# A decode-step kernel on one core: the last row of w2 brought in for 80 of its 128 partitions by two transfers of 40

## The chip, the cores and the metric

The kernel runs on one core of one Trainium2 chip. The metric is the device time of one execution in microseconds (us). The kernel before the change takes 133.50 us, the median of three runs (133.49, 133.50 and 133.52). Smaller is better.

## What is computed

Two branches read the same layer-normalized vector and are added to the input. Branch A is attention for one new token per batch row (B = 2) over the last 2048 positions of a cache; branch B is a dense layer with a squared ReLU. Cut to what matters:

```python
xn = _layernorm(x)                       # x: (2, 1, 576)
# A: 32 query heads, 16 kv heads, head size 128, window W = 2048
q = xn @ wq                              # wq: 576 x 4096
p = softmax(q . k[Sk-W:] * Dh**-0.5)
A = (p . v[Sk-W:]) @ wo                  # wo: 4096 x 576
# B: F = 4608
r = relu(xn @ w1 + b1)                   # w1: 576 x 4608
Bo = (r * r) @ w2 + b2                   # w2: 4608 x 576
return x + A + Bo
```

All inputs are bf16. The k and v windows and the four weight matrices make 53.6 MB, which have to be read from memory once.

## The kernel before

**The work and its stages.** The 2 x 16 cached heads are worked off as eight units (`NU`) of four kv heads each; unit u takes head group `u // 2` of batch row `u % 2`. A unit needs one k tile and one v tile, each 128 partitions by 8192 elements (2 MB). They sit in a pool of six buffers (`kvpool`, tag `kv`), so that a load waits until PE has finished with an older tile. `step(u)` (line 388) transposes k on PE in eight groups of four matmuls (`transposes`, line 261; ACT and DVE take turns copying the result to SBUF, lines 273 and 275), forms the scores, takes the softmax, and in between multiplies the probabilities of unit u - 2 with v (`pv`, line 315). Before the steps the kernel normalizes x, loads wq and forms q (`q_rows`, `q_place`). After step 6 `mlp_h` (line 357) forms h from w1, squares its ReLU, and transposes it: 18 small PE transposes into `hp`, and eight copies of 32 partitions, shared by DVE and ACT, into `hT_sb` (lines 379 to 386). Then come the last step (unit 7), the last two `pv`, and the output products.

**The output products.** `wo` and `w2` are laid over the 128 partitions so that each partition holds whole rows. For w2, line 208 gives half x, partition p and row r: `w2_rows[x, p, r]` is row x*2304 + 18*p + r of w2, 576 numbers. A product for one r is therefore a pair of PE matmuls (`out_acc`, line 216, one for each half of the 576 columns) with the 128 x 2 activations `hT_sb[:, x, r, :]` as weights and the 128 x 288 pieces of w2 as data, summed in PSUM (`out_ps`). The first half of w2 is `w2a` (18 rows). The second half is `w2b` (rows 0 to 8, in a buffer of the kv pool) and `w2c` (rows 9 to 17), which line 76 cuts into three transfers: rows 9 to 14 (864 KB), rows 15 and 16 (288 KB) and row 17 (144 KB). The final loop (line 468) takes the 18 pairs in order; after row 8 it has three matmuls on `spin_ps` whose result is used by nobody.

**What sets the order.** All big loads are issued by SP, in the order of the program text, and every transfer of 128 partitions lies on all 16 DMA engines, 8 partitions on each. `keep_in_program_order` (lines 93 and 96) holds PE to the order of the text, so a PE instruction that waits holds up all that come behind it. DVE, ACT and POOL are ordered by the tile scheduler. Each DMA counts on one of eight semaphores in turn, and its issue waits for the transfer that used the semaphore before. ACT issues the small loads: x (line 126), b1 in two transfers of four rows (line 420) and b2 (line 421). At the end ACT copies the sum out of PSUM (line 478), and ACT and SP each write half of the result (lines 479 and 480). Ahead of that, line 477 lets ACT write two rows of w2b into the output, which the real write overwrites later.

Of the kernel before, what the change touches and what calls it, by code (L numbers as in the profile page):

```python
# [8 lines left out]
F32 = mybir.dt.float32  # L9
BF16 = mybir.dt.bfloat16  # L10
# [6 lines left out]
def kernel(  # L17
# [14 lines left out]
    nc = tc.nc  # L32
    P = 128
    B, Sq, D = A_x.shape
# [39 lines left out]
    FR = L1 // P  # L74
    assert HW == 32 * FR and QH * 2 == NC and NC * WC == 32
    W2P = [(9, 15), (15, 17), (17, 18)]
    R9 = 9
    HD = D // 2
    RO = 32 + B
    RP = 96 + B  # L80
# [3 lines left out]
    kvpool = ctx.enter_context(tc.tile_pool(name="kvpool", bufs=6))  # L84
# [3 lines left out]
    work = ctx.enter_context(tc.tile_pool(name="work", bufs=2))  # L88
    keep = ctx.enter_context(tc.tile_pool(name="keep", bufs=2))
    psum = ctx.enter_context(tc.tile_pool(name="psum", bufs=1, space=bass.MemoryType.PSUM))  # L90

    def matmul(*a, **k):
        tc.keep_in_program_order(nc.tensor.matmul(*a, **k))  # L93
# [5 lines left out]
    out2d = out.rearrange("b s d -> (b s) d")  # L99
# [50 lines left out]
    ident = const.tile([P, P], BF16, name="ident")  # L150
# [29 lines left out]
    for t0, half, k0, n, pc in ((0, 0, 0, NK, 0), (0, 1, 0, NK, 1), (1, 0, 1, NK - 1, 1), (1, 1, 0, NK - 1, 0)):  # L180
# [11 lines left out]
                          in_=own[:].unsqueeze(2).to_broadcast([P, NC, WC]))  # L192
    in_s = const.tile([P, NS], F32, name="in_s")
    nc.vector.tensor_reduce(out=in_s[:], in_=ident[:].rearrange("p (g s c) -> p s g c", s=NS, c=NC), axis=AX.XY,
                            op=ALU.add)
# [8 lines left out]
                          in_=ident[0:2 * NG4, 0:2 * NG4].rearrange("p (x g) -> p x g", g=NG4).unsqueeze(3)  # L204
                          .to_broadcast([2 * NG4, 2, NG4, B]))

    b1_sb = const.tile([2 * NG4, HW], BF16, name="b1_sb")
    w2_rows = B_w2.rearrange("(x p r) n -> x p (r n)", x=2, r=FR)


    w2c_sb = w2pool.tile([P, (FR - R9) * D], BF16, name="w2c")

    out_ps = psum.tile([RO, HD], F32, tag="out", name="out_ps")
    nc.vector.memset(out_ps[:], 0.0)

    def out_acc(lhsT, rhs, o, start=False, stop=False, acc=out_ps, base=0):
        for i in range(2):
            p = base + 32 * i
            matmul(acc[p:p + B, :], lhsT=lhsT, rhs=rhs[:, o * D + i * HD:o * D + (i + 1) * HD], start=start,
                   stop=stop, skip_group_check=True, tile_position=(0, p))  # L220
# [40 lines left out]
    def transposes(u, g):  # L261
        k_f = k_tiles[u][:].bitcast(F32)
        kT_ps = psum.tile([P, JG * P], BF16, tag="kT", bufs=3, name=f"kT_ps_{u}_{g}")
        kT_f = kT_ps[:].bitcast(F32)
        for i in range(JG // 2):
            j = g * JG // 2 + i
            transpose(out=kT_f[:, i * P:(i + 1) * P], in_=k_f[:, j * P:(j + 1) * P], identity=ident_f[:])
        t, o = divmod(g, TG)
        if o == 0:
            kT_tiles[(u, t)] = ktpool.tile([P, TG * JG * P], BF16, tag="kT_sb", name=f"kT_{u}_{t}")  # L270
        kT = kT_tiles[(u, t)][:, o * JG * P:(o + 1) * JG * P]
        if g % 2 == 0:
            nc.scalar.copy(out=kT, in_=kT_ps[:])  # L273
        else:
            nc.vector.tensor_copy(out=kT, in_=kT_ps[:])  # L275
# [35 lines left out]

    ws = const.tile([P, WR, B], BF16, name="ws")
    hT_sb = const.tile([P, 2, FR, B], BF16, name="hT_sb")

    def pv(u, part, parts):
        n = NJJ // parts
        if part == 0:
            o_tiles[u] = psum.tile([P, NS * Dh], F32, tag="o", name=f"o_ps_{u}")
        v = v_tiles[u][:].rearrange("p (t j s d) -> p j t s d", t=NT, s=2, d=Dh)
        for j in range(part * n, (part + 1) * n):  # L320
            g = j % 4
            matmul(o_tiles[u][32 * g:32 * (g + 1), :], lhsT=pT_tiles[u][:, j, :], rhs=v[:, j], start=(j < 4),
                   stop=(j >= NJJ - 4), skip_group_check=True, tile_position=(0, 32 * g))
        if part == parts - 1:
            pT_tiles.pop(u)

    def pv_end(u):
        tq, b = divmod(u, B)
        o_ps = o_tiles.pop(u)
        o1 = o1_tiles.pop(u)  # L330
        for k in range(NS):
            kw = dict(out=o1[:, 0:Dh], in0=o_ps[:, k * Dh:(k + 1) * Dh])
            if k == 0:
                nc.vector.tensor_scalar(scalar1=in_s[:, 0:1], scalar2=None, op0=ALU.mult, **kw)  # L334
            else:
                nc.vector.scalar_tensor_tensor(scalar=in_s[:, k:k + 1], in1=o1[:, 0:Dh], op0=ALU.mult, op1=ALU.add,  # L336
                                               **kw)

        def fin():
            op = psum.tile([P, Dh + 1], F32, tag="op", name=f"op_ps_{u}")  # L340
            pp = slice(32 * tq, 32 * (tq + 1))
            matmul(op[pp, :], lhsT=of_h[:], rhs=o1[:], start=True, stop=True, skip_group_check=True,
                   tile_position=(0, 32 * tq))
            linv = work.tile([P, 1], F32, tag="linv", name=f"linv_{u}")
            nc.vector.reciprocal(out=linv[pp, :], in_=op[pp, Dh:Dh + 1])
            om_t = work.tile([P, Dh], F32, tag="om", name=f"om_{u}")
            om = om_t[pp, :].rearrange("p (q r) -> p q r", r=WR)
            nc.vector.scalar_tensor_tensor(out=om, in0=op[pp, 0:Dh].rearrange("p (q r) -> p q r", r=WR),
                                           scalar=linv[pp, 0:1], op0=ALU.mult, op1=ALU.mult,
                                           in1=own_c[pp, :].unsqueeze(2).to_broadcast([32, WC, WR]))  # L350
            with nc.allow_low_precision(reason="sums of one term and zeros"):
                nc.vector.tensor_reduce(out=ws[pp, :, b], in_=om.rearrange("p q r -> p r q"), axis=AX.X,  # L352
                                        op=ALU.add)

        return fin

    def mlp_h(w1_sb):
# [20 lines left out]
        for a in range(2):  # L378
# [3 lines left out]
            for g in range(NG4):  # L382
# [2 lines left out]
                cp(out=hT_sb[pp, :, a * nr:(a + 1) * nr, :].rearrange("p x r b -> p r x b"),  # L385
                   in_=hp[pp, :, 32 * g:32 * g + 2 * B].rearrange("p r (x b) -> p r x b", b=B))

    def step(u):
        fin = None
        w = u - 2  # L390
        with_pv = w >= 0
        for g in range(NG):
            transposes(u, g)
            if with_pv and g == 1:
                pv(w, 0, 2)
            if with_pv and g == 2:
                pv(w, 1, 2)
                fin = pv_end(w)
            if g == TG + 1:
                scores(u, 0)  # L400
            if g == TG + 2 and fin:
                fin()
        scores(u, 1)
        softmax(u)

    def pv_all(u):
        pv(u, 0, 1)
        pv_end(u)()
# [7 lines left out]
    softmax(0)  # L416
    load_v(2)
    b1_rows = B_b1.rearrange("(x n) -> x n", n=HW)
    for i0, i1 in ((0, 4), (4, 8)):
        nc.scalar.dma_start(out=b1_sb[i0:i1, :], in_=b1_rows[i0:i1, :])  # L420
    nc.scalar.dma_start(out=xb_sb[B:B + 1, :], in_=B_b2.rearrange("(o n) -> o n", o=1))
    step(1)
    load_k(4)
    out_acc(sel_b[:], xb_sb, 0, start=True)
    for u in range(2, NU - 1):
        step(u)
        if u + 1 < NU - 2:
            load_v(u + 1)
        if u == 4:
            w1_sb = issue_flat(B_w1, "w1")  # L430
        if u + 3 < NU:
            load_k(u + 3)
        if u == 5:
            for v in (NU - 2, NU - 1):
                load_v(v)
    mlp_h(w1_sb)
    wo_sb = issue_flat(A_wo, "wo")
    w2a_sb = w2pool.tile([P, FR * D], BF16, name="w2a")
    w2b_sb = kvpool.tile([P, R9 * D], BF16, tag="kv", name="w2b")
    nc.sync.dma_start(out=w2a_sb[:], in_=w2_rows[0])  # L440
    nc.sync.dma_start(out=w2b_sb[:], in_=w2_rows[1, :, 0:R9 * D])
    for r0, r1 in W2P:
        nc.sync.dma_start(out=w2c_sb[:, (r0 - R9) * D:(r1 - R9) * D], in_=w2_rows[1, :, r0 * D:r1 * D])
    step(NU - 1)
    pv_all(NU - 2)
    pv_all(NU - 1)
    pre_ps = psum.tile([RP, HD], F32, tag="sc", bufs=2, name="pre_ps")
    nc.vector.memset(pre_ps[:], 0.0)
    pre_sb = work.tile([P, HD], F32, tag="t1", name="pre_sb")
    nc.gpsimd.memset(pre_sb[:], 0.0)  # L450
# [13 lines left out]
    for i in range(2):  # L464
        p = 64 + 32 * i
        matmul(out_ps[32 * i:32 * i + B, :], lhsT=ident_f[:, p:p + B], rhs=pre_sb[:], start=False, stop=False,
               skip_group_check=True, tile_position=(0, 32 * i))
    for r in range(FR):
        w, o = (w2b_sb, r) if r < R9 else (w2c_sb, r - R9)
        out_acc(hT_sb[:, 1, r, :], w, o, stop=(r == FR - 1))  # L470
        if r == R9 - 1:
            for _ in range(3):
                matmul(spin_ps[0:B, :], lhsT=ws[:, 0, :], rhs=wo_sb[:, 0:512], start=True, stop=True,
                       skip_group_check=True)

    fin_sb = work.tile([RO, HD], BF16, tag="fin", name="fin_sb")
    nc.scalar.dma_start(out=out2d[:, 0:HD], in_=w2b_sb[0:B, 0:HD])
    nc.scalar.copy(out=fin_sb[:], in_=out_ps[:])
    nc.scalar.dma_start(out=out2d[:, 0:HD], in_=fin_sb[0:B, :])
    nc.sync.dma_start(out=out2d[:, HD:D], in_=fin_sb[32:RO, :])  # L480
# [30 lines left out]
```

## Time and profile before

| | us |
|---|---|
| median of three runs | 133.50 |
| the profiled execution, its time | 133.6 |
| its span, first to last instruction | 131.7 |
| PE busy (matmuls) | 84.6 |
| DVE busy | 63.1 |
| ACT busy | 46.6 |
| mean granted clock of TensorE | 0.883 |
| DMA, MB and mean rate over the span | 53.74 MB, 408 GB/s |

The profile is of one execution. Busy times are shares of the span; matmuls are pipelined, so that their busy time overlaps. "PEld" is the load of weights into TensorE. In the chain of waits each piece is what the next one waited for; a DMA piece in it runs from the issue to the landing, so it holds the time in the queue behind earlier transfers too. The windows view gives for a stretch of time the busy time of an engine, the granted clock (1.00 is full speed) and the mean busy share of the 16 DMA engines. The trace also keeps the start, length and size of every DMA packet, and the moment at which each engine's part of a transfer was counted on its semaphore.

### The profile page before, as it was taken

What the parts mean: (1) busy time and instruction counts of PE and PEld (TensorE: products, weight loads), DVE (VectorE), ACT (ScalarE), POOL (GpSimd) and SP (SyncE); (2) the same over time, 40 slices, a digit from 0 to 9 for tenths busy, and PEclk for the clock granted to TensorE, in tenths of its full rate; (3) what the DMA queues carried; (4) which work ended last, traced back from release to release, by engine and by line L of the source; (5) the groups of instructions that cost most, each with busy time, mean ns of one, the idle gap of its engine ahead of it and who ended that gap; (6) DMA issues with size and microseconds to landing.
All of it is one profiled execution on the core that took longest, in us unless ns stands there. A gap on an engine that the chain in (4) does not pass through costs nothing.

```text
span 131.7 us, 2025 instructions
## 1 busy us (share of the span) xinstructions
PE 84.6 (64%) x818; PEld 46.3 (35%) x818; DVE 63.1 (48%) x176; ACT 46.6 (35%) x68; POOL 4.2 (3%) x14
## 2 busy tenths in 40 slices
PE   0040767985599687699687797003919974629782
PEld 0010236553346353345353353002507631205341
DVE  6760034555447677457677496400073487560000
ACT  6700019497255185265085283200015452000101
POOL 2000000010100100100100100100010001000000
PEclk9999999999779999859999999955586899655799
DMA  4999999999999999999999999999999989899970
GB/s 118 480 419 420 418 443 418 448 418 423 445 413 438 423 443 428 413 458 413 443 423 411 458 490 403 408 431 428 413 443 418 504 381 504 382 416 403 400 286 1
DMA packets 3643, 53.74 MB, mean 408 GB/s; under 512 B 418, under 2 KB 563, under 8 KB 819
## 3 DMA queue, kind: packets, MB, share of 16 engines
q1 hardware_dynamic: 3604, 53.61, 95.6%
q8 instruction: 6, 0.10, 0.3%
q10 hardware_dynamic: 30, 0.02, 0.0%
q14 instruction: 3, 0.02, 0.0%
HBM read 53.62 MB, written 0.00 MB: 407 GB/s over the span
## 4 chain that ended last, share of the span: by engine, by line
DMA 74%; PE 15%; ACT 5%; issue 1%; SPq 1%; DVE 1%; ACTq 0%; DVEq 0%
DMA w<-in_B_w_dram 24%; DMA w2c<-in_B_w_dram 23%; DMA k<-in_A_k_cache_dram 17%; DMA wq<-in_A_wq_dram 10%; PE kT_ps L96 5%; PE h_ps L93 3%; ACT kT L273 3%; PE q_ps L93 2%; PE sc_ps L93 2%; PE o_ps L93 1%; PE out_ps L93 1%; ACT L305 1%; SPq L120 1%; DVE qrow L241 1%; ACT qrow L241 0%
## 5 line engine op out<-in xcount | busy, mean ns | idle before, releaser
L96 PE MATMUL kT_ps<-ident_f,k 128*128 128x128 f32 x256 | 39.0, 295 | 6.7 <-DMA k<-in_A_k_cache_dram 4.2
L273 ACT COPY kT<-kT_ps 128x1024 bf16<-128x1024 bf16 x32 | 31.8, 1012 | 15.3 <-PE kT_ps L96 15.3
L96 PEld LDWEIGHTS kT_ps<-ident_f,k 128*128 128x128 f32 x256 | 29.3, 149 | 21.8 <-issue 7.4
L275 DVE COPY kT<-kT_ps 128x1024 bf16<-128x1024 bf16 x32 | 21.8, 682 | 6.4 <-PE kT_ps L96 5.9
L93 PE MATMUL sc_ps<-kT,qz 128*32 128x512 bf16 x128 | 9.8, 384 | 6.1 <-DVE kT L275 5.5
L305 ACT ACTIVATE p<-sc_ps,bias 128x512 bf16<-128x512 f32 x8 | 5.5, 687 | 21.5 <-DVE gown L301 21.4
L93 PE MATMUL o_ps<-v,pT 128*32 128x512 bf16 x128 | 12.2, 466 | 0.0
L93 PE MATMUL h_ps<-w,xnT 128*4 128x288 bf16 x72 | 4.5, 442 | 8.8 <-DMA w<-in_B_w_dram 8.8
L93 PEld LDWEIGHTS <-xnT 128*4 128x4 bf16 x108 | 3.5, 117 | 18.3 <-issue 15.3
L336 DVE SCALAR_TENSOR_TENSOR o<-o_ps,in_s,o 128x128 f32<-128x128 f32 x24 | 8.2, 344 | 0.4
L308 DVE STREAM_TRANSPOSE pT<-p 128x512 bf16<-128x512 bf16 x8 | 5.7, 709 | 5.6 <-ACT p L305 5.6
L376 DVE TENSOR_TENSOR hrow<-t 100x1152 bf16<-100x1152 f32 x2 | 2.6, 1354 | 10.5 <-ACT t L374 10.5
L93 PE MATMUL q_ps<-wq,xnT 128*4 128x512 bf16 x36 | 4.2, 622 | 5.4 <-DMA wq<-in_A_wq_dram 4.0
L294 DVE TENSOR_REDUCE m<-sc_ps 128x1 f32<-128x512 f32 x8 | 5.5, 691 | 3.4 <-PE sc_ps L93 3.4
L93 PE MATMUL op_ps<-o,of_h 128*32 128x129 f32 x16 | 3.4, 299 | 4.6 <-DVE o L336 4.6
L298 POOL PARTITION_ALL_REDUCE gmax<-m x8 | 2.9, 365 | 92.2 <-DVE m L296 92.2
L93 PEld LDWEIGHTS <-qz 128*32 128x32 bf16 x128 | 2.0, 94 | 9.9 <-DVE kT L275 7.6
L334 DVE TENSOR_SCALAR o<-o_ps,in_s 128x128 f32<-128x128 f32 x8 | 2.7, 343 | 5.3 <-PE o_ps L93 5.3
L96 PE MATMUL pro_ps<-ident,xn_sb 2*128 2x2 bf16 x5 | 0.9, 181 | 6.8 <-DVE xn_sb L171 6.5
L241 ACT CAST qrow<-q_ps 100x512 bf16<-100x512 f32 x1 | 0.6, 585 | 12.1 <-DVE qrow L241 12.1
L463 ACT COPY pre_sb<-pre_ps 34x288 f32<-34x288 f32 x1 | 0.4, 393 | 12.6 <-PE pre_ps L93 12.6
L93 PE MATMUL out_ps<-wo,ws 128*2 128x288 bf16 x32 | 4.0, 441 | 1.1 <-DVE ws L352 1.1
(76 smaller groups left out, 61.4 us busy)
## 6 DMA issues: line engine op xcount, KB each, us to landing
k<-in_A_k_cache_dram SPq DMA_DIRECT2D x8, 2048.0 KB, 25.6
v<-in_A_v_cache_dram SPq DMA_DIRECT2D x8, 2048.0 KB, 22.8
w<-in_B_w_dram SPq DMA_DIRECT2D x1, 5184.0 KB
wo<-in_A_wo_dram SPq DMA_DIRECT2D x1, 4608.0 KB
wq<-in_A_wq_dram SPq DMA_DIRECT2D x1, 3584.0 KB, 12.9
w2a<-in_B_w_dram SPq DMA_DIRECT2D x1, 2592.0 KB
w2b<-in_B_w_dram SPq DMA_DIRECT2D x1, 1296.0 KB, 29.2
wq<-in_A_wq_dram SPq DMA_DIRECT2D x1, 1024.0 KB, 4.8
```

The lines of the kernel that those rows point to most:

```text
L93: tc.keep_in_program_order(nc.tensor.matmul(*a, **k))
L96: tc.keep_in_program_order(nc.tensor.transpose(*a, **k))
L241: cp(out=qrow[:, k * QW:(k + 1) * QW].rearrange("p (i a d) -> p i a d", a=2, d=Dh), in_=q_ps[0:RB, k * QW // 2:(k + 1) * QW // 2].rearrang ...
L273: nc.scalar.copy(out=kT, in_=kT_ps[:])
L275: nc.vector.tensor_copy(out=kT, in_=kT_ps[:])
L294: nc.vector.tensor_reduce(out=m1[:], in_=sc_ps[:], axis=AX.X, op=ALU.max)
L298: nc.gpsimd.partition_all_reduce(gmax[:], m2[:], channels=P, reduce_op=ReduceOp.max)
L305: nc.scalar.activation(out=p_sb[:], in_=sc_ps[:], func=ACT.Exp, bias=bias[:, 0:1], scale=scale, accum_out=o1[:, Dh:Dh + 1])
L308: nc.vector.transpose(out=pT[:].rearrange("p j r -> p (j r)"), in_=p_sb[:])
L334: nc.vector.tensor_scalar(scalar1=in_s[:, 0:1], scalar2=None, op0=ALU.mult, **kw)
L336: nc.vector.scalar_tensor_tensor(scalar=in_s[:, k:k + 1], in1=o1[:, 0:Dh], op0=ALU.mult, op1=ALU.add, **kw)
L376: nc.vector.tensor_tensor(out=h4[:, :, k * HB:(k + 1) * HB], in0=t4, in1=t4, op=ALU.mult)
```

## The change

Row 17 of the second half of w2 no longer arrives in one transfer of 128 partitions. Partitions 80 to 127 (48 of them) are still loaded into `w2c`; the other 80 rows are brought by two transfers of 40 into partitions 0 to 39 of a spare place at the end of `w2b` (`w2s_sb`). Their source is walked as 5 groups of 8 partitions that lie 16 apart. Both are issued ahead of the transfer of rows 15 and 16. The activations have to follow: two 0/1 matrices (`pick`, cut from the identity) move the 80 activations of row 17 to partitions 0 to 39 (`hs_ps`, two PE products at the end of `mlp_h`, then a DVE copy to `hs_sb`). The final loop gets two more pairs of matmuls ahead of row 15, for `hs_sb`; the pair of row 17 remains with all 128 partitions, and its 80 unloaded ones are set to zero by POOL at the start. b1 is loaded by one transfer of 8 rows in place of two of 4, and the early write of line 477 is gone.

```diff
+    GS = 5
+    PS = 8 * GS
+    nc.gpsimd.memset(w2c_sb[0:2 * PS, (FR - R9 - 1) * D:], 0.0)
...
+    hs_sb = work.tile([PS, 2, B], BF16, tag="hs", bufs=1, name="hs_sb")
+    pick = work.tile([P, 2, PS], BF16, tag="pick", bufs=1, name="pick")
+    nc.vector.tensor_copy(out=pick[:].rearrange("p s (g i) -> p s g i", g=GS),
+                          in_=ident[:, 0:2 * PS].rearrange("p (g s i) -> p s g i", g=GS, s=2))
...
+        hs_ps = psum.tile([PS, 2, B], F32, tag="op", name="hs_ps")
+        for i in range(2):
+            matmul(hs_ps[:, i, :], lhsT=pick[:, i, :], rhs=hT_sb[:, 1, FR - 1, :], start=True, stop=True, skip_group_check=True)
+        nc.vector.tensor_copy(out=hs_sb[:], in_=hs_ps[:])
...
-    for i0, i1 in ((0, 4), (4, 8)):
-        nc.scalar.dma_start(out=b1_sb[i0:i1, :], in_=b1_rows[i0:i1, :])
+    nc.scalar.dma_start(out=b1_sb[:], in_=b1_rows[:, :])
...
-    w2b_sb = kvpool.tile([P, R9 * D], BF16, tag="kv", name="w2b")
+    w2b_sb = kvpool.tile([P, (R9 + 2) * D], BF16, tag="kv", name="w2b")
+    w2s_sb = w2b_sb[0:PS, R9 * D:]
...
     for r0, r1 in W2P:
-        nc.sync.dma_start(out=w2c_sb[:, (r0 - R9) * D:(r1 - R9) * D], in_=w2_rows[1, :, r0 * D:r1 * D])
+        p0 = 2 * PS if r1 == FR else 0
+        if r1 == FR - 1:
+            src = w2_rows[1, 0:2 * PS, r1 * D:].rearrange("(g s i) n -> s g i n", g=GS, s=2)
+            for i in range(2):
+                nc.sync.dma_start(out=w2s_sb[:, i * D:(i + 1) * D], in_=src[i])
+        nc.sync.dma_start(out=w2c_sb[p0:, (r0 - R9) * D:(r1 - R9) * D], in_=w2_rows[1, p0:, r0 * D:r1 * D])
...
         w, o = (w2b_sb, r) if r < R9 else (w2c_sb, r - R9)
+        if r == W2P[1][0]:
+            for i in range(2):
+                out_acc(hs_sb[:, i, :], w2s_sb, i)
         out_acc(hT_sb[:, 1, r, :], w, o, stop=(r == FR - 1))
...
-    nc.scalar.dma_start(out=out2d[:, 0:HD], in_=w2b_sb[0:B, 0:HD])
```

More of the change, by code (lines that the diff above doesn't have):

```diff
@@ L438 @@
     w2a_sb = w2pool.tile([P, FR * D], BF16, name="w2a")
-    w2b_sb = kvpool.tile([P, R9 * D], BF16, tag="kv", name="w2b")
+    w2b_sb = kvpool.tile([P, (R9 + 2) * D], BF16, tag="kv", name="w2b")
+    w2s_sb = w2b_sb[0:PS, R9 * D:]
     nc.sync.dma_start(out=w2a_sb[:], in_=w2_rows[0])
-    nc.sync.dma_start(out=w2b_sb[:], in_=w2_rows[1, :, 0:R9 * D])
+    nc.sync.dma_start(out=w2b_sb[:, 0:R9 * D], in_=w2_rows[1, :, 0:R9 * D])
     for r0, r1 in W2P:
-        nc.sync.dma_start(out=w2c_sb[:, (r0 - R9) * D:(r1 - R9) * D], in_=w2_rows[1, :, r0 * D:r1 * D])
+        p0 = 2 * PS if r1 == FR else 0
[4 more added lines that the diff above has]
+        nc.sync.dma_start(out=w2c_sb[p0:, (r0 - R9) * D:(r1 - R9) * D], in_=w2_rows[1, p0:, r0 * D:r1 * D])
     step(NU - 1)
```

## The prediction, on record before the changed kernel ran

> **What bounds the kernel now.** I read the page first, then the chain of waits, then the windows of the last microseconds. The page has the DMA engines full from start to end, and the chain that ended last is mostly DMA:
>
> ```profile
> DMA  4999999999999999999999999999999989899970
> ...
> q8 instruction: 6, 0.10, 0.3%
> q10 hardware_dynamic: 30, 0.02, 0.0%
> ...
> DMA 74%; PE 15%; ACT 5%; issue 1%; SPq 1%; DVE 1%; ACTq 0%; DVEq 0%
> ```
>
> So nothing on PE, ACT or DVE counts before the last bytes of w2 arrive, unless it makes PE late for them. The end of the chain of waits:
>
> ```profile
> 96.95 30.81 DMA w2c<-in_B_w_dram
> 127.75 0.04 issue
> 127.80 1.36 PE out_ps L93 x18
> 129.16 0.02 issue
> 129.18 0.39 ACT fin_sb L478
> ```
>
> The landing that the end hangs on is that of the **first** piece of w2c (rows 9 to 14), at 127.75; from there PE runs its nine pairs (x18) nearly without a break. Timelines cut to one engine show how nearly (a group is listed whole, or from the window's first instruction on):
>
> ```profile
> 125.73 1.27 PE L93 MATMUL out_ps<-w2b,hT_sb 128*2 128x288 bf16 x18 [0.21 <-DMA w2b<-in_B_w_dram]
> 126.83 0.81 PE L93 MATMUL spin_ps<-wo,ws 128*2 128x512 bf16 x3
> 127.80 0.29 PE L93 MATMUL out_ps<-w2c,hT_sb 128*2 128x288 bf16 x2 [0.15 <-DMA w2c<-in_B_w_dram]
> 128.85 0.29 PE L93 MATMUL out_ps<-w2c,hT_sb 128*2 128x288 bf16 x2
> ```
>
> Nine pairs on w2b, all landed, take 1.27 with 0.283 for the last pair alone: (1.27 - 0.283) / 8 = 0.123 from pair to pair. At that pace the pair of row 17, eight after row 9, would start at 127.80 + 0.98 = 128.78. It started at 128.85. **The wait for the transfer that the change cuts up is worth 0.07 to 0.08 us**, no more. Its landing count in the trace is complete at 128.81.
>
> Why does it land that late? The windows view (us, PE busy, granted clock, DMA share, GB/s):
>
> ```profile
> 126.40:126.80 0.40, 0.40 (x10) 1.00 0.99 379
> 126.80:127.20 0.40, 0.40 (x6) 1.00 0.53 210
> 127.20:127.60 0.40, 0.40 (x3) 1.00 0.48 180
> 127.60:128.00 0.40, 0.24 (x5) 1.00 0.38 147
> 128.00:128.40 0.40, 0.40 (x10) 1.00 0.29 104
> 128.40:128.80 0.40, 0.40 (x10) 1.00 0.01 3
> ```
>
> The 16 engines don't end together: 0.53 is some eight engines, 0.29 some five. Following the packets (each starts where the last one of its engine ends) gives the ends of row 17: eight engines at 126.66 to 127.05, two at 127.54 and 127.59, six at 128.09, 128.24, 128.31, 128.43, 128.44 and 128.49. The late ones are those that also carried instruction fetches: the six 16 KB packets of q8 (started at 28.9, 48.6, 68.2, 83.0, 105.0, 123.3) hit six different engines and put each some 1.5 behind; two 8 KB packets of q14 put two others 0.75 behind.
>
> **The change, part by part.** *DMA.* A packet of one 1152-byte row starts 0.047 after the one before. Late engines not used by the 40-row transfers carry 3 rows of row 17 in place of 8: 5 x 0.047 = 0.235 less, so 128.49 becomes 128.25 and the landing 128.81 becomes 128.58. An engine that takes 8 rows of each 40-row transfer carries 16 + 3 in place of 8, and two more count packets: 11 x 0.047 + 0.012 = 0.53 more. How many engines these transfers use, no row shows. The nearest: a transfer of 128 rows ends with 16 count packets, one for each engine used, and ACT's transfers of 1, 2 and 4 rows (q10) with 1, 2 and 4; so the ends are one engine (80 x 0.047 = 3.8 us on it) and sixteen (nothing won, nothing lost). I take five engines with 8 rows each, as the source is walked as five groups of eight, the way four rows went to four engines; the four that the b1 transfers used ended at 126.77, 126.83, 127.54 and 127.59, so plus 0.53 they end by 128.12, still inside the others. [...]
>
> *PE's tail.* Two more pairs ahead of row 15: 2 x 0.123 = 0.245. Row 9 starts at 127.80 as before, since nothing ahead of the first w2c piece is changed; its six pairs end their starts as before, the two new ones follow, rows 15 and 16, and row 17 starts at 127.80 + 10 x 0.123 = 129.03, with its landing (128.58) long past. Before it was 128.85: **+0.17**. That the new pairs have 40 partitions instead of 128 I count as nothing, since PE streams 288 columns either way. They wait for the two small transfers, which follow the first w2c piece: on an engine that ended it at 126.49 their 16 rows end by 127.3, plus 0.35 from packet to count 127.6; cover 0.9 before 128.53.
>
> *PE at the end of `mlp_h`.* The two small products wait for all eight copies into hT_sb, and unit 7's transposes stand behind them. Before, those began at 99.69, while the copies ran until 100.56 (DVE) and one ACT copy came at 101.90, behind a kT copy; in the new order ACT has it ahead, so at about 100.6. With two products of 0.1 to 0.2 the transposes start near 101.0: 1.3 late. At that point the clock is half; from 103.01 it was full, so work pushed past it takes half as long, and 0.65 remains. Again from 118.4 to 123.5 (half clock, wo products): 0.65 shrinks to about 0.3. PE's waits further on are 0.25 (w2a), 0.21 (w2b) and 0.15 (w2c): cost 0. Without that cover up to 1.3.
>
> *The rest.* pick: about 0.2 (DVE copies and compares of that width take 0.16 to 0.29) in DVE's 0.68 idle ahead of rstd: 0. The POOL memset, between 0.34 (pre_sb) and 0.74 (qz), pushes the qz memset to about 2.0; qz is first written by DVE at 19.2: 0. hs_sb's copy, 0.18 like hT_sb's, ahead of a kT copy for which DVE waited 1.1: 0. SP issues two more transfers (0.43 each) and by the turn of semaphores the last one waits for a later v tile; all that is 15 us and more before their bytes are due: 0. b1 in one transfer: ACT issues one less, first use at 91: 0, and at most 0.06 on an engine. The dropped write: ACT stood idle from there to 129.18: 0; if it had warmed the path, the last ACT issue (0.25) might take SP's 0.32, and SP's half lands last anyway.
>
> **Sum.** Profiled execution 133.6 = span 131.7 + 1.9 around it; +0.17 gives 133.77. The median is 0.1 below the profiled execution, so 133.50 + 0.17 = 133.67, **133.7**. What a measurement of this kernel can tell from no change is about 0.2%, 0.27 us: I forecast a small loss inside that.
>
> **Rivals.**
> 1. *The late transfer was the bound after all: faster.* For: q1 alone fills 95.6% of the 16 engines over the span (page, part 3). Against: the wait before row 17 is 0.08, and the landing at 127.75, with eight pairs behind it, is untouched. With the new pairs hidden the most is -0.08, 133.4; for -0.27 the first w2c piece too would have to land 0.4 earlier, on all six late engines (they ended it at 126.99 to 127.38). 0.08.
> 2. *The fifth engine is a late one: slower.* By the count above four engines are known and none is of the six late; of the other twelve, half are. Then its row 17 ends 0.53 later, 128.6 to 129.0, counts 0.35 later, and PE starts 0.04 after: 129.0 to 129.4 against 128.85, so +0.17 to +0.56, mostly +0.5: 134.0. It decides as soon as that engine ends row 17 after 128.6. If the fetches go round the engines in turn, the fifth is less likely hit than a coin toss: 0.25.
> 3. *The small transfers hinder other engines.* They write partitions 0 to 39, which in the large transfers belong to several engines. If two engines that write neighbouring partitions share a way in, each of up to 8 packets steals 0.047 from a late engine still on the first w2c piece: +0.38 on 127.75, with the 0.17 133.5 + 0.55 = 134.05. Nothing in the trace shows such sharing. [...] 0.10.
> 4. *PE comes late* from the stall in `mlp_h`. If the clock stays half from 103.0 to 106.4 (it rose after windows with PE busy 2.81 of 3.41 and more, not after 2.30; here about 2.5), 1.3 stays, and with the waits above 0.1 to 0.3 may reach the end: 133.9. 0.07.
>
> **Numbers.** Forecast 0.50, rivals 0.08, 0.25, 0.10, 0.07. The range leaves out half of rival 1 and the upper ends of 2 and 3: 133.45 to 134.1. Faster by over 0.2%: 0.08. Within: 0.50 and the lowest part of rival 2, 0.52. Slower: 0.40.
>
> **What would show it.** Right: the last windows empty earlier, no wait before row 17, 22 matmuls from 127.8 at 0.123 a pair, the cast 0.17 later. The stall: unit 7's transposes from 101.0, wo products from 118.4 to 119.5, w2b still begun on its landing. Rival 2: a wait before row 15 or 17; rival 3: the first w2c piece landing after 127.9. Wrong altogether: that first landing moving by more than 0.1 either way.

## The result: 134.44 us, 0.7% slower, and the profile after

The changed kernel takes 134.44 us (median of six runs, 134.17 to 134.80) against 133.50: ratio 1.0072, interval 1.0055 to 1.0088. The forecast was 133.7, with a range up to 134.1. The profiled execution took 134.39, its span is 132.4. Each trace below is of one execution, and the six runs lie 0.6 apart, so a tenth read from a single trace is no more than that trace's.

The end of the chain of waits (start, length, what), which before was one DMA piece and PE's last pairs, now lies on PE throughout:

```profile
125.38 0.40 ACT pre_sb L480
125.78 0.04 issue
125.83 1.76 PE out_ps L95 x22
127.58 0.64 PE spin_ps L95 x3
128.22 1.55 PE out_ps L95 x22
129.78 0.02 issue
129.80 0.39 ACT fin_sb L497
```

ACT's cast starts at 129.80, 0.62 later than before. PE's timeline of the same stretch:

```profile
126.31 1.27 PE L95 MATMUL out_ps<-w2b,hT_sb 128*2 128x288 bf16 x18
127.41 0.81 PE L95 MATMUL spin_ps<-wo,ws 128*2 128x512 bf16 x3
128.02 0.94 PE L95 MATMUL out_ps<-w2c,hT_sb 128*2 128x288 bf16 x12
128.89 0.41 PE L95 MATMUL out_ps<-w2b,hs_sb 40*2 40x288 bf16 x4
129.23 0.53 PE L95 MATMUL out_ps<-w2c,hT_sb 128*2 128x288 bf16 x6
```

No line has an idle time behind it: PE never waits here. It comes to w2b at 126.31, 0.62 after that landed (125.69 in the trace); before, it waited for it and began at 125.73. And the landing of the first w2c piece, counted complete at 127.75 before, is now at 127.98. PE gets there at the same moment, so two separate delays meet in one start, 128.02 instead of 127.80. From there the pairs run with two breaks: the six pairs of rows 9 to 14 would give way after 0.74, at 128.76, but the pairs with 40 partitions start at 128.89, and row 15 at 129.23 and not at 129.14. (Of the first break's 0.13, 0.04 belongs to the last spin: the second matmul of row 9's pair begins only at 128.06. In the kernels below, where PE waits for the landing, this break is 0.09 to 0.10.) Row 17 no longer waits.

The same windows as before (us, PE busy, granted clock, DMA share, GB/s):

```profile
126.40:126.80 0.40, 0.40 (x10) 1.00 0.85 277
126.80:127.20 0.40, 0.40 (x12) 1.00 0.57 199
127.20:127.60 0.40, 0.40 (x9) 1.00 0.68 231
127.60:128.00 0.40, 0.40 (x3) 1.00 0.50 196
128.00:128.40 0.40, 0.40 (x9) 1.00 0.22 75
128.40:128.80 0.40, 0.40 (x10) 1.00 0.00 0
```

The last window is empty, as forecast. But from 127.2 to 127.6 the engines are more busy than before (0.68 against 0.48) and move fewer bytes for it: 231/0.68 = 340 GB/s at full share, before 180/0.48 = 375. Some packets take longer, which the packet records show one by one (below).

**The account of the profiled executions**, 134.39 - 133.6 = 0.79: start of the first w2c pair +0.22; two more pairs +0.245; the two breaks +0.22; the wait before row 17 -0.08; that is 0.61, and the cast is 0.62 later. The time from the last landing to the end of the span is 0.90 instead of 0.83, and what lies outside the span 1.99 instead of 1.89. The profiled execution of before is 0.10 above its median, that of after 0.05 below, which makes the rest of the 0.94.

### The profile page after: what moved, and what is told of

Read it like the earlier page. It is cut to its first block, busy times and chain, and to the rows that moved or that the text cites. A ratio compares the mean times of both kernels' runs of the same rounds, so it can differ in the third digit from the quotient of the medians.

```text
span 132.4 us, 2039 instructions
## 1 busy us (share of the span) xinstructions
PE 84.4 (64%) x824; PEld 48.2 (36%) x824; DVE 63.4 (48%) x178; ACT 46.7 (35%) x68; POOL 4.7 (4%) x15
## 4 chain that ended last, share of the span: by engine, by line
DMA 51%; PE 31%; DVE 8%; ACT 5%; issue 2%; POOLq 0%; SPq 0%; ACTq 0%
DMA w<-in_B_w_dram 25%; DMA k<-in_A_k_cache_dram 17%; PE kT_ps L98 10%; DMA wq<-in_A_wq_dram 10%; PE out_ps L95 6%; PE h_ps L95 3%; PE sc_ps L95 3%; PE q_ps L95 2%; PE o_ps L95 2%; ACT kT L276 2%; DVE hrow L383 2%; DVE o L343 2%; PE hp L98 1%; ACT L308 1%; PE op_ps L95 1%
## 5 line engine op out<-in xcount | busy, mean ns | idle before, releaser
L98 PE MATMUL kT_ps<-ident_f,k 128*128 128x128 f32 x256 | 39.8, 301 | 7.4 <-DMA k<-in_A_k_cache_dram 6.2
L98 PEld LDWEIGHTS kT_ps<-ident_f,k 128*128 128x128 f32 x256 | 30.5, 152 | 21.7 <-issue 12.6
L95 PE MATMUL o_ps<-v,pT 128*32 128x512 bf16 x128 | 11.0, 430 | 0.0
L244 DVE CAST qrow<-q_ps 100x512 bf16<-100x512 f32 x1 | 0.7, 690 | 8.2 <-PE q_ps L95 8.2
```

What stands on the lines that cost most here:

```text
L98: tc.keep_in_program_order(nc.tensor.transpose(*a, **k))
L244: cp(out=qrow[:, k * QW:(k + 1) * QW].rearrange("p (i a d) -> p i a d", a=2, d=Dh), in_=q_ps[0:RB, k * QW // 2:(k + 1) * QW // 2].rearrang ...
```

## The experiments

Theory after reading the profile: three causes. The small transfers hinder the late engines, those that are still on the first w2c piece when the others are done (rival 3 of the prediction); PE is late from `mlp_h` (rival 4), beside the first and hidden behind it; and the tail costs 0.36 in place of 0.17, because of the switch to 40 partitions and back. The rival theories: the tail alone, or the two small edits (b1, the early write). Results in one table; each ratio is to runs of the kernel before on the same chip. "Pair" is the start of the first pair on w2c, "end" the time from the last landing to the end of the span, both of the profiled execution. The profiled execution of before is 0.1 above its usual median. The runs of before beside the a kernels have a median of 133.67, those beside the others 133.48 to 133.53; the times expected below were worked out from 133.5.

| kernel | ratio, interval | first w2c landing | pair | cast | end |
|---|---|---|---|---|---|
| before | 1 | 127.75 | 127.80 | 129.18 | 0.83 |
| after | 1.0072, 1.0055 to 1.0088 | 127.98 | 128.02 | 129.80 | 0.90 |
| a1_stall | 1.0029, 1.0018 to 1.0040 | 127.68 | PE late | 129.81 | 0.82 |
| a2_dma | 1.0038, 1.0026 to 1.0051 | 128.36 | 128.40 | 129.71 | 0.90 |
| a3_pairs | 1.0098, 1.0083 to 1.0114 | 128.63 | 128.68 | 130.41 | 0.83 |
| a4_late | 1.0070, 1.0058 to 1.0083 | 128.25 | 128.29 | 130.03 | 0.89 |
| b1_misc | 1.0016, 1.0007 to 1.0025 | 127.60 | 127.64 | 129.04 | 0.96 |
| f1_nowrite | 1.0009, 1.0000 to 1.0017 | 127.63 | 127.67 | 129.07 | 0.89 |
| c1_ownpart | 1.0018, 1.0008 to 1.0027 | 128.02 | 128.06 | 129.40 | 0.93 |
| c3_pairs40 | 1.0032, 1.0019 to 1.0045 | 127.71 | 127.75 | 129.49 | 0.83 |
| c4_pairs128 | 1.0018, 1.0009 to 1.0027 | 127.64 | 127.68 | 129.24 | 0.83 |
| d1_both | 1.0057, 1.0044 to 1.0069 | 127.85 | 127.89 | 129.63 | 0.93 |
| d2_ownonly | 1.0096, 1.0081 to 1.0112 | 127.90 | 127.94 | 129.68 | 0.94 |
| e1_best | 1.0045, 1.0033 to 1.0058 | other pieces | | 129.05 | 1.09 |
| e3_three | 1.0024, 1.0014 to 1.0035 | other pieces | | 129.11 | 0.89 |
| g1_code | 1.0008, 0.9999 to 1.0017 | 127.74 | 127.78 | 129.18 | 0.83 |

### One part at a time

**a1_stall**: before, with `pick`, `hs_ps` and `hs_sb` as in the change, their result used by nobody.

```diff
...
+        hs_ps = psum.tile([PS, 2, B], F32, tag="op", name="hs_ps")
+        for i in range(2):
+            matmul(hs_ps[:, i, :], lhsT=pick[:, i, :], rhs=hT_sb[:, 1, FR - 1, :], start=True, stop=True, skip_group_check=True)
+        nc.vector.tensor_copy(out=hs_sb[:], in_=hs_ps[:])
```

> The kernel before, with the 0/1 matrices, the two small products at the end of mlp_h and their DVE copy added; nothing uses their result, transfers and output products are those of before. If PE's path is the cause (theory 1: the wait for all eight copies holds up the transposes of unit 7, and PE comes late to the first w2c piece), the transposes start at about 101.2 instead of 99.7, PE begins the w2c pairs 0.1 to 0.4 after their landing at 127.75, and the time is 133.6 to 133.9. If the small transfers on the DMA engines are the cause (theory 2), 133.5.

+0.36 (134.03 against 133.67). The transposes of unit 7 start at 101.02. PE's lines at the end:

```profile
126.27 0.65 PE L95 MATMUL out_ps<-pre_sb,ident_f 128*2 128x288 f32 x4 [0.56 <-ACT pre_sb L474]
126.75 1.27 PE L95 MATMUL out_ps<-w2b,hT_sb 128*2 128x288 bf16 x18
```

w2b had landed at 125.63, and before its pairs began at 125.73: PE is 1.0 late here, more than expected, and the spins and the wait for w2c cover only a part. The stall alone outlasts all the cover that the prediction counted on.

**a2_dma**: the change without the pick, the products and the two pairs; what remains are the transfers, b1 and the early write.

```diff
...
-        if r == W2P[1][0]:
-            for i in range(2):
-                out_acc(hs_sb[:, i, :], w2s_sb, i)
```

> The changed kernel without the 0/1 matrices, the products and the two extra pairs: the transfers, the zeroed rows, b1 and the dropped write stay, so the 80 rows of w2 are loaded but left out of the sum. Theory 1: PE arrives as before and the wait before row 17 is gone, 133.4 to 133.5. Theory 2: the first w2c piece lands at about 127.98 instead of 127.75 with packets stretched around 126.5 to 127.5, row 17 starts at 128.03 + 0.98 = 129.0, and the time is 133.65 to 133.75.

+0.49 (134.16), and a landing later than the 127.98 expected: PE is on time and waits 0.62 for the first piece, which lands at 128.36:

```profile
126.96 0.81 PE L95 MATMUL spin_ps<-wo,ws 128*2 128x512 bf16 x3
128.40 1.27 PE L95 MATMUL out_ps<-w2c,hT_sb 128*2 128x288 bf16 x18 [0.62 <-DMA w2c<-in_B_w_dram]
```

So here transfers that are queued behind the first piece delay it: it lands at 128.36, 127.75 in before. What the packet records show of it comes in the next part.

**a3_pairs**: before, with two more pairs of 40 partitions on zeros ahead of row 15, and the small `hs_sb` among the constants.

```diff
+    hs_sb = const.tile([PS, 2, B], BF16, name="hs_sb")
+    nc.gpsimd.memset(hs_sb[:], 0.0)
...
+        if r == W2P[1][0]:
+            for i in range(2):
+                out_acc(hs_sb[:, i, :], w2b_sb[0:PS, :], i)
```

> The kernel before with two extra pairs of 40 partitions ahead of row 15 (zero activations, first rows of w2b as data), all else as before. By the pace of 0.123 alone: +0.245 less the wait of 0.08, so +0.17, 133.67. With the two breaks seen at the switch between 128 and 40 partitions (0.13 and 0.09): +0.39, 133.9. Theory 2: 133.5.

134.94, far too much. Not the pairs: w1 already lands at 91.55 (before 91.04). The added constant moved every large tile by 32 bytes (w2c, for one, from address 168960 to 168992), and from 20 us on the 16 KB packets take 614 ns at the median instead of 611, some 621. It was redone as c3_pairs40.

**c3_pairs40, c4_pairs128**: the same with `hs_sb` in the work pool, which moves no large tile; once 40 partitions, once 128.

```diff
-    hs_sb = const.tile([PS, 2, B], BF16, name="hs_sb")
+    hs_sb = work.tile([PS, 2, B], BF16, tag="hs", bufs=1, name="hs_sb")
```

and for c4_pairs128 also

```diff
-    hs_sb = work.tile([PS, 2, B], BF16, tag="hs", bufs=1, name="hs_sb")
+    hs_sb = work.tile([P, 2, B], BF16, tag="hs", bufs=1, name="hs_sb")
...
-                out_acc(hs_sb[:, i, :], w2b_sb[0:PS, :], i)
+                out_acc(hs_sb[:, i, :], w2b_sb[:], i)
```

> The kernel before with two more pairs of matmuls ahead of row 15, on 40 partitions, with activations of zero and w2b as data (as a3_pairs, but the small activation tile is in the work pool and not among the constants, where it moved the places of the large tiles and every 16 KB packet took 614 ns in place of 611). Theory (switching the weights from 128 to 40 partitions and back costs PE about 0.2, the pairs 0.245, the wait for row 17 gives 0.07 back): the last matmul 0.36 to 0.39 later from the first w2c pair than before, 133.9 to 134.0; DMA as before. If the switch were free: +0.17, 133.75.

> As c3_pairs40, with the two added pairs on all 128 partitions. Theory (the switch is what breaks the pace): 22 matmuls at 0.123 us a pair without a break, +0.17, 133.75; 0.15 to 0.22 less than c3_pairs40. If the breaks belong to the change of the data tile and not to the number of partitions, it takes the same as c3_pairs40.

+0.44 and +0.20. PE's last lines, c3_pairs40 first:

```profile
127.75 0.90 PE L95 MATMUL out_ps<-w2c,hT_sb 128*2 128x288 bf16 x12 [0.15 <-DMA w2c<-in_B_w_dram]
128.58 0.41 PE L95 MATMUL out_ps<-w2b,hs_sb 40*2 40x288 bf16 x4
128.92 0.53 PE L95 MATMUL out_ps<-w2c,hT_sb 128*2 128x288 bf16 x6
```

```profile
127.68 0.90 PE L95 MATMUL out_ps<-w2c,hT_sb 128*2 128x288 bf16 x12 [0.15 <-DMA w2c<-in_B_w_dram]
128.41 0.41 PE L95 MATMUL out_ps<-w2b,hs_sb 128*2 128x288 bf16 x4
128.66 0.54 PE L95 MATMUL out_ps<-w2c,hT_sb 128*2 128x288 bf16 x6
```

From the first pair to the added ones 0.83 against 0.73, from there to row 15 0.34 against 0.25: each change of the number of partitions costs 0.09 to 0.10. The chain's PE piece is 1.72 and 1.53 long, in before 1.36. With 128 partitions the prediction's +0.17 is met to the hundredth (1.53 - 1.36); the switch adds 0.19.

**b1_misc, f1_nowrite**: before, with both small edits, and with the early write dropped alone (the last line of the diff).

```diff
-    for i0, i1 in ((0, 4), (4, 8)):
-        nc.scalar.dma_start(out=b1_sb[i0:i1, :], in_=b1_rows[i0:i1, :])
+    nc.scalar.dma_start(out=b1_sb[:], in_=b1_rows[:, :])
...
-    nc.scalar.dma_start(out=out2d[:, 0:HD], in_=w2b_sb[0:B, 0:HD])
```

> The kernel before with only the two small edits of the change that touch neither w2 nor PE: b1 in one transfer of 8 rows, and the early write of two rows of w2b left away. Theory (the loss comes from the small w2 transfers and from PE's added work): nothing, within 0.1 us of the kernel before; no packet of the first w2c piece longer than 262 ns except where an instruction fetch falls. Rival (these edits delay the end: the early write had made the last write quick, or one b1 transfer of eight rows puts eight engines back): +0.2 us or more, to be seen between the cast and the last landing, or in the first w2c landing.

> The kernel before with only the early write of two rows of w2b left away; b1 in two transfers as before. If the early write had made the last write quicker or steadier: +0.1 to +0.2, as b1_misc (133.67 against 133.48). If b1's single transfer makes b1_misc's 0.19: within 0.05 of the kernel before.

+0.19 and +0.13, with nothing later up to the cast. b1_misc was expected to cost nothing; f1_nowrite came out in its range, though not for the reason given there. What the traces show is behind the last landing: 0.96 and 0.89 instead of 0.83. There SP waits for the semaphores in five steps, always in the same order, 0.06 to 0.07 apart in the semaphore records; the eight of the DMAs are spread over them. In the traces of before and after every transfer takes the next of the eight in turn, so the number of transfers in the whole program settles on which ones the output's two writes count. Before, these are in the last two steps (130.73 and 130.91, the landings at 130.71 and 130.89). With one transfer less, one step is left after the last landing, with two less there are two: +0.067 and +0.135. (The other 0.06 of each median lies within the intervals and is not explained.) In the change itself two added and two dropped transfers cancel; its 0.90 comes from the order of the two halves (ACT's lands last, on the last but one step), so that one step is left over.

### Why the first piece lands later

In the packet records a packet of the first w2c piece (6912 bytes) takes 262 ns. The table counts those longer than 1.1 times that; a fetch that falls on a packet shows as one of over 700 (one each in after, a4_late, c1_ownpart and d1_both), and the packet behind it is long too. "Behind w2b" is the time from the landing of w2b to that of the first w2c piece.

| kernel | of 128 packets of 6912 bytes | of 128 of 2304 bytes (93 ns) | longest of these, ns | behind w2b |
|---|---|---|---|---|
| before | 0 | 0 | 93 | 2.06 |
| after | 10, up to 369 ns | 22 | 244 | 2.29 |
| a2_dma | 11, up to 388 ns | 17 | 153 | 2.54 |
| a4_late | 24, up to 424 | 40 | 238 | 2.54 |
| c1_ownpart | 2, at a fetch | 0 | 95 | 2.26 |
| d1_both | 2, at a fetch | 0 | 93 | 2.19 |
| d2_ownonly | 1, at a fetch | | | 2.32 |

The last column is 2.05 or 2.06 in the seven kernels that load all of row 17 in one transfer (before, a1, b1, f1, c3, c4, g1), and so shows the delay best. In a2_dma the long packets lie on the six late engines alone, the ones that carried a 16 KB fetch (on one of the six the longest is 286), from the fifth packet on, while other engines already run the small transfers.

**c1_ownpart**: a2_dma with the same 80 rows in four transfers of 20, to other partitions.

```diff
-            src = w2_rows[1, 0:2 * PS, r1 * D:].rearrange("(g s i) n -> s g i n", g=GS, s=2)
-            for i in range(2):
-                nc.sync.dma_start(out=w2s_sb[:, i * D:(i + 1) * D], in_=src[i])
+            src = w2_rows[1, 0:2 * PS, r1 * D:].rearrange("(g s i) n -> s g i n", g=GS, s=4)
+            for i in range(4):
+                p1 = 32 * (i % 2)
+                nc.sync.dma_start(out=w2b_sb[p1:p1 + 4 * GS, (R9 + i // 2) * D:(R9 + i // 2 + 1) * D], in_=src[i])
```

> [...] Theory (in a2_dma the packets of the first w2c piece were stretched from 262 to as much as 388 ns because two engines met at the same partitions): no stretched packets but for fetches, the first landing back at 127.7 to 127.9, and 0.3 to 0.5 us less than a2_dma, 133.6 to 133.8 in the same session. Rival (small packets, their count or their source in memory disturb the stream, wherever they land): ten or more stretched packets and a first landing of 128.2 or later, 134.1.

133.72, ratio 1.0018 against a2_dma's 1.0038, and no stretched packet but at a fetch. As many rows, as many bytes, five engines as before (five counts for each transfer): what differs is where they land, partitions 0 to 19 and 32 to 51 in place of 0 to 39, and that there are four transfers of 20 rows and not two of 40. Which of the two differences ended the stretching, no run shows, nor which engine writes which partitions; that two engines met at the same partitions in a2_dma stays a guess.

Nor is the delay gone. c1_ownpart's first piece lands at 128.02, outside the 127.7 to 127.9 expected, and 2.26 behind w2b; d1_both and d2_ownonly, below, have the same transfers and 2.19 and 2.32, and after itself, with its long packets, has no more than 2.29. In d1_both the last packet of the piece ends at 127.30 (before 127.38) and its last count comes at 127.85 (before 127.75). So it is shown that small transfers queued behind the first piece delay it, by 0.13 to 0.26 in four transfers of 20 and by 0.23 to 0.48 in two of 40, and that the long packets come with the two of 40. By what path one engine holds up another, and what delays the counts where no packet is long, is not.

### Both late chains, taken away singly and together

**a4_late**: the change, with the products for `hs_sb` after the last step's scores, so that unit 7's transposes don't wait. **d2_ownonly**: the change with c1_ownpart's transfers (`hs_sb` then has 52 partitions, 12 of them zero). **d1_both**: both.

```diff
-        hs_ps = psum.tile([PS, 2, B], F32, tag="op", name="hs_ps")
...
     step(NU - 1)
-    pv_all(NU - 2)
+    pv(NU - 2, 0, 1)
+    hs_ps = psum.tile([PS, 2, B], F32, tag="kT", bufs=3, name="hs_ps")
...
+    pv_end(NU - 2)()
```

> The whole change, but the two small products stand after unit 7's scores and the next pv products instead of at the end of mlp_h. If the stall is what made PE late and nothing else matters, the transposes of unit 7 start at 99.7 and the time falls from 134.44 to about 133.9 (the tail's 0.39 stays). If the DMA is late too (theory 2), PE waits for the first w2c piece until 127.98 and the time is about 134.1 to 134.2, that is, the stall by itself costs little on top.

> As d1_both, but the products stay at the end of mlp_h, as in the change: the transfers are mended alone. Theory (two late chains meet at the first w2c pair, the DMA and PE, and the stall in mlp_h by itself makes PE that late): the time stays near that of the change, 134.3 to 134.5, w2b's pairs begin 0.5 or more after their landing, and PE comes to the first w2c pair after its landing. Rival (the stall hardly counts, the landing alone sets the end): 134.1, as d1_both.

> The whole change with both causes taken away: the products for the 80 activations come after the last step's scores (as in a4_late, so PE isn't held up in mlp_h), and the 80 rows go by four transfers of 20 into partitions 0 to 19 and 32 to 51 (as in c1_ownpart, so no packets are stretched); the two added pairs then have 52 partitions, 12 of them zeros. Theory (what is left is PE's tail: two pairs 0.245 and the switch to fewer partitions and back 0.19): c1_ownpart's 133.72 plus 0.41 (tail 1.72 in place of 1.31), 134.1; first w2c landing 127.8 to 128.1, tail 1.7. Rival (the neighbouring partitions were not the whole of a4_late's lateness): 134.4 or more, with ten or more stretched packets of the first w2c piece.

134.60, 134.70 and 134.21. Neither cure helps alone, as two chains run side by side: a4_late has PE on time, and waits for a landing at 128.25 (127.98 and 134.1 to 134.2 were expected); d2_ownonly has the landing at 127.90, but PE reaches w2b at 126.10, 0.5 after it landed, and the chain of waits runs through PE again. A line of each, a4_late first:

```profile
128.29 0.90 PE L95 MATMUL out_ps<-w2c,hT_sb 128*2 128x288 bf16 x12 [0.57 <-DMA w2c<-in_B_w_dram]
126.10 1.27 PE L96 MATMUL out_ps<-w2b,hT_sb 128*2 128x288 bf16 x18
```

With both the chain is the DMA's again, with no stretched packets, and PE's tail of 1.72 remains. Here d1_both:

```profile
126.80 0.81 PE L96 MATMUL spin_ps<-wo,ws 128*2 128x512 bf16 x3
127.89 0.90 PE L96 MATMUL out_ps<-w2c,hT_sb 128*2 128x288 bf16 x12 [0.28 <-DMA w2c<-in_B_w_dram]
128.72 0.41 PE L96 MATMUL out_ps<-w2b,hs_sb 52*2 52x288 bf16 x4
129.06 0.53 PE L96 MATMUL out_ps<-w2c,hT_sb 128*2 128x288 bf16 x6
```

The intervals of d1_both and of the change overlap; the gain of 0.2 rests on the medians and on these lines. d2_ownonly came out slower than expected (134.3 to 134.5), which is not explained; its trace is of its fastest run, 134.41 of up to 134.94, and doesn't show what the others lost.

### A version after the theory, and the end of the program

**e1_best**: small transfers as in c1_ownpart but ahead of w2a, their pairs while ACT copies `pre_sb`, products late, w2c in four pieces (rows 9 to 11, 12 to 14, 15 and 16, 48 rows of 17), b1 and the early write as before. **e3_three**: the same with b1 in five transfers instead of two. The core of e1_best, against d1_both, and then e3_three's edit:

```diff
-    W2P = [(9, 15), (15, 17), (17, 18)]
+    W2P = [(9, 12), (12, 15), (15, 17), (17, 18)]
...
...
     nc.scalar.copy(out=pre_sb[64:RP, :], in_=pre_ps[64:RP, :])
+    for i in range(2):
+        out_acc(hs_sb[:, i, :], w2s_sb, i)
...
```

```diff
-    for i0, i1 in ((0, 4), (4, 8)):
+    for i0, i1 in ((0, 2), (2, 4), (4, 6), (6, 7), (7, 8)):
```

> A version after the theory, to see whether the idea can pay: the 80 rows in four transfers of 20 into partitions 0 to 19 and 32 to 51, issued ahead of w2a, so that they are long there; their two pairs on PE while ACT copies pre_sb, where PE sat idle for 0.56; the products for their activations late, as in a4_late; the rest of w2c cut into rows 9 to 11, 12 to 14, 15 and 16, and the 48 rows of row 17; b1 and the early write as in the kernel before. Theory: no stretched packets in w2c; the tail is then set by the last landing, 0.1 to 0.24 earlier than 128.81: 133.3 to 133.45. Rival (early engines become late ones by their 16 rows, or the stream is disturbed at another place): 133.6 or more.

> e1_best with b1 loaded by five small transfers in place of two, nothing else: three transfers more, at a time when nobody waits for them. At the end of the program SP waits for the eight DMA semaphores one after the other, 0.065 each; in e1_best the output's two writes counted on the fourth and fifth of them, so that four waits came after the last landing, and the span ended 1.09 after it, 0.83 in the kernel before, where they counted on the last two. Theory: three more transfers move the writes back to the last two semaphores, the span ends 0.83 after the last landing, and the time falls by 0.2 to 0.27 against e1_best (ratio to before 1.0045 there), to a ratio near 1.0025. Rival (the end of the program doesn't matter, e1_best is slow by something in the stream): the same as e1_best, ratio 1.004 to 1.005.

e1_best: 134.16, missed by 0.7, though its cast is at 129.05, 0.13 earlier than before (in the fastest of its runs, 133.85; the other four are 0.1 to 0.5 longer). Five transfers more than before put the output's writes into the first two of SP's five steps, so four follow the last landing, and the span ends 1.09 after it. e3_three, with three transfers more, has them in the last two steps, with one step left over as in after (0.89, 0.83 expected): 133.83, ratio 1.0024 where 1.0025 was expected. Splitting b1's load into three more transfers, which moves no other bytes, made the kernel 0.3 faster, of which the traces show 0.20 behind the last landing. Neither beats the kernel before.

**g1_code**: before, with only `pick` and the late products.

```diff
-    pv_all(NU - 2)
+    pv(NU - 2, 0, 1)
+    hs_ps = psum.tile([PS, 2, B], F32, tag="kT", bufs=3, name="hs_ps")
...
+    nc.vector.tensor_copy(out=hs_sb[:], in_=hs_ps[:])
+    pv_end(NU - 2)()
```

> The kernel before with only the 0/1 matrices, and the two products and the copy of the 80 activations, placed late as in a4_late, their result used by nobody: no transfer changed, no pair added, no stall in mlp_h. Theory (in the kernels with these products an instruction fetch of 8 KB shows after the last instruction, and up to 0.25 more lies outside the span; that is a price of the added code): 133.55 to 133.75, ratio 1.0005 to 1.002, and time less span 2.0 to 2.15 in several runs, where it is 1.87 to 1.9 in the kernel before. Rival (what lies outside the span doesn't come from the code): time less span 1.87 to 1.9 and the time of the kernel before within 0.05.

133.62 against 133.53, with an interval that reaches 1. The span is the same; time less span is 1.92 to 2.16 in eleven runs, mean 2.03, and 1.84 to 1.94, mean 1.90, in the runs of before: 0.13 for code that costs nothing inside the span. The other runs agree: the means of the eight kernels with these products are 1.95 (after) to 2.06, those of all others 1.87 to 1.90. All kernels with these products (after, a1, a4, d1, d2, e1, e3, g1) show an 8 KB instruction fetch at 133.6 to 134.7, after the last instruction; none of the others does. That this fetch is the reason is likely, not shown: in a1_stall's and d1_both's profiled executions it is there, and time less span is 1.87 to 1.89.

## Why the prediction was wrong, step by step

- **What bounds the kernel**: right. The first w2c piece and the pairs behind it set the end, and row 17's wait was worth no more than 0.08; so there was nothing to gain.
- **Five engines for the small transfers**: right, five counts each. Rival 2, the fifth engine a late one, did not happen: of the five the latest count is 127.84.
- **Row 17's landing at 128.58**: wrong, 128.87 (before 128.81). The 0.235 saved was eaten by the later first piece (+0.23) and by stretched packets behind it. It cost nothing, as PE came later.
- **"Row 9 starts at 127.80 as before, since nothing ahead of the first w2c piece is changed"**: the first failed step. The order in each engine's queue was unchanged, but engines that are done go on to the small transfers while the six late ones are still on the first piece (in after the first small packet starts at 125.70, and the last packet of the piece ends at 127.53), which then lands 0.23 later, against w2b as well (2.29 and 2.06). By the prediction's own sign, a first landing moved by more than 0.1, it was wrong altogether. In a2_dma, ratio 1.0038, in c1_ownpart 1.0018, with 0.07 and 0.11 us of end in them. This is rival 3 in what it forecast (small transfers that hinder other engines, +0.38; the traces have 0.23 in after, 0.48 in a4_late and a2_dma, against w2b), while its way in shared by neighbours isn't shown. It was held at 0.10 because before showed no such sharing. It could hardly show it: there no small transfer into w2's tiles runs beside the stream.
- **"+0.17" for two pairs less the wait**: right (c4_pairs128, 1.53 - 1.36). **"40 partitions instead of 128 I count as nothing"**: the second failed step; it counted the data columns, which are the same, and not the change in the number of partitions. 0.19 (c3_pairs40 against c4_pairs128).
- **Stall in `mlp_h`, cost 0**: the third failed step. The chain of waits of after:

```profile
100.88 0.19 ACT hT_sb L392
101.07 0.04 issue
101.11 0.20 PE hs_ps L95 x2
101.31 1.90 PE kT_ps L98 x8
```

  The last ACT copy ends at 101.07, the two products follow, and the transposes began at 101.24 in the timeline (101.0 said), 1.55 late. That was to shrink by half as the clock rose at 103.0. It didn't rise. The changes of the clock in after lie at 106.83, 117.07 and 123.89, 10.24 and 6.82 apart, three and two times 3.41, and in before at 103.01, 113.25 and 123.49, 10.24 apart: in each trace such a grid lies elsewhere. Windows on each kernel's own grid (us, PE busy, granted clock, DMA share, GB/s), before, after and then a4_late, whose grid is within 0.03 of after's and which is without the stall:

```profile
99.60:103.01 3.41, 3.41 (x23) 0.50 1.02 437
103.01:106.43 3.42, 3.42 (x34) 1.00 1.17 496
```

```profile
100.00:103.42 3.42, 2.51 (x17) 0.50 0.95 407
103.42:106.83 3.41, 3.41 (x23) 0.50 1.19 513
```

```profile
99.98:103.39 3.41, 3.41 (x21) 0.50 1.06 453
103.39:106.80 3.41, 3.41 (x35) 1.00 1.13 485
```

  The stall left PE idle for 0.9, so its window to 103.42 was busy for 2.51 only, and the next one stayed at half clock: 23 instructions in place of 35. In these windows 1.00 came after one that was busy for 3.41 of 3.41 (before, a4_late), and 0.50 after one of 2.51 (after); that the busy time is what decides is the author's reading of them. In the three traces with the stall the clock rose at 105.00 (a1_stall), 106.60 (d2_ownonly) and 106.83, in all others at 101.2 to 104.9. How busy is enough, the traces don't settle: before rose after a window of 2.81, c3_pairs40 not after one of 2.90. The wo products began at 120.29 instead of 118.39, 1.9 late, and PE was 0.62 late at w2b. Not all of the 1.9 is the stall's: in the traces without it they begin at 117.8 to 119.3, in those with it at 119.6 to 120.3. Rival 4 had this very condition ("about 2.5") and got 0.07. The forecast took the clock of before as given for work that it had moved. By itself the stall costs 0.36; in the change it stands beside the DMA's delay, and taking it out alone gains nothing (a4_late).
- **The rest, 0**: pick, memset and copies, yes up to the cast. Outside it not: 0.07 at the semaphores, where ACT's half landed last and not SP's as the prediction said (131.50 and 131.32), and 0.06 to 0.13 outside the span. The b1 edit and the dropped write cost 0.19 by themselves, 0.135 of it since they shift the semaphores; beside two added transfers that cancels.
- **The sum** missed 0.2 of switch, 0.2 to 0.3 of landing and stall (side by side), and 0.2 at the end; the rest, 0.15, is how the two profiled executions lie to their medians. The rivals were treated as alternatives; 3 and 4 came together.

## What to carry to other kernels

Here small transfers slowed one that is ahead of them in the queue, in a2_dma on engines that they don't use (the landing came 0.13 to 0.48 later behind w2b): look at the length of equal packets and at the time from one landing to the next, not only at the order. A stall can cost more than its length: here the clock stayed at half for 3.41 more after 0.9 of idle PE, so work out the busy time of the windows that the stall empties before letting later waits pay for it. And when a kernel is down to tenths of a microsecond, its end is part of it: here the number of transfers decided how many semaphore waits, of 0.06 to 0.07 each, followed the last landing.

## What the runs showed of the chip, unexpected

- Packets of engines that still stream were stretched from 262 ns to 291 and up to 424 by two transfers of 40 rows of 1152 bytes into partitions 0 to 39 (after, a2_dma, a4_late), and not by the same rows in four transfers into partitions 0 to 19 and 32 to 51 (c1_ownpart, d1_both, d2_ownonly); the landing came later with either (2.19 to 2.54 behind w2b in place of 2.06).
- 32 bytes mattered: in a3_pairs large tiles shifted by 32 bytes had 16 KB packets of 614 ns (up to 621) instead of 611, and the stream was 0.5 late at 91 us and 0.8 at w2b (126.50 against 125.69).
- A matmul on 40 or 52 partitions behind one on 128, and the way back, cost 0.09 to 0.10 each at 0.123 a pair (c3_pairs40, d1_both); with 128 throughout there was no break (c4_pairs128).
- Each of SP's five semaphore steps at the end takes 0.06 to 0.07, and only those behind the last landing counted: 0.83 from there to the end of the span in before, 0.89 in f1_nowrite, 0.96 in b1_misc, 1.09 in e1_best.
